# A Fourier attention layer and a mixture of experts on one core: two pairs of frequency bins are worked as one group, with the inverse length-64 stage for both at once

## The chip, the cores and the metric

The kernel runs on one core of a Trainium2 chip. The metric is the device time of one execution in microseconds (us). Each core has five engines that run their own instruction streams: PE (TensorE, matrix products; its weight loads are listed as PEld), DVE (VectorE), ACT (ScalarE), POOL (GpSimd) and SP (SyncE, which here issues the direct DMAs).

## The reference, cut to what matters

```python
def _attn_ref(x, w_r, w_i, b_r, b_i):            # x: 8 x 2496 x 256
    X = np.fft.rfft(x, axis=1)
    Yr = X.real @ w_r - X.imag @ w_i + b_r
    Yi = X.real @ w_i + X.imag @ w_r + b_i
    lam = 0.01
    Yr = np.sign(Yr) * np.maximum(np.abs(Yr) - lam, 0.0)   # Yi the same
    return np.fft.irfft(Yr + 1j * Yi, n=2496, axis=1)

def _moe_ref(x, modality_id, w_gate, modality_bias, w1, w2):   # x: 19968 x 256
    logits = x @ w_gate + modality_bias[modality_id]
    e_idx = np.argmax(logits, axis=1)            # one of 8 experts per token
    ...
    for e in range(E):
        h = np.maximum(x[mask] @ w1[e], 0.0)     # mask = e_idx == e
        out[mask] = gate_w[mask, None] * (h @ w2[e])
```

## The kernel before

The transform of length 2496 is split as 39 x 64. For each of the eight batches the attention stage first takes the length-39 DFT over x in 11 chunks (`s1_chunk`, L265 to L267; each chunk of x is split into a rounded high part on ACT or DVE and a remainder `x1l` on DVE, `s1_split`, L246 and L247) and sends it through DRAM (`scr`). Of the 39 bins 20 are kept, and they are worked two at a time: ten **pairs** per batch. A pair p goes through four steps on PE:

- `s2_pair` (L299): the length-64 DFT; ACT and DVE then cut the result into Us (a sum), Xh and Xl (L306 to L309).
- `mix_shared` (L329): two matmuls of the sums Us, on top of a bias that ACT has put into the PSUM tile `mx` (`mix_bias`, L317); then DVE adds the other bias and writes the second half of the tile (L330). The profile records each of these float32 matmuls twice.
- `mix_own` (L337): 12 matmuls of Xh and Xl into both halves of `mx`, so its first one has to wait for L330. Then `shrink`, the soft threshold (ACT L344, DVE L345).
- `is2_pair` (L360): the inverse length-64 stage, 16 matmuls that use half the rows of the array each (eight for either half), into two PSUM tiles, which DVE and ACT copy to `z` (L363), 256 wide.

In the loop over p of `build` the order is: sums of pair p+1, length-64 DFT of p+2, own half of p+1, inverse stage of p. After the ten pairs come the **pivots** of the batch: 22 rounds of `pivot` (L373, then ACT L378 and DVE L379) and `is1` (the inverse length-39 stage, L385 to L387, result copied by ACT or DVE, L388), with the s1 chunks of batch b+2 between them. A pair stage and its pivots make up the batch; the next batch's first sums stand behind the last pivot.

Beside that run: the **routing** of the batch before (`Route`: logits, softmax and ranks on DVE, its two sets of small matmuls on PE), which ends in 22 indirect DMAs that scatter a batch's tokens to `xs` in DRAM (`scatter`, L548, on POOL), one after each pair or two pivots; and the split of the experts' weights (`SplitWeights.step`: load `wr` on SP, rounded copy `wh` on ACT L994, remainder `wl` on POOL or DVE L995, two stores on SP, and the load for a later step). In the last two batches `rt.scatter(J)` issues whatever scatters are left, and behind those of batch 6's pivots `fence` (L592), a DMA on SP, waits for all of them before any expert may read `xs`.

Then come the experts (`Experts`): per tile of 256 tokens load `xt` from `xs`, `prep` (transposition on DVE L795, rounded copy on ACT L799, remainder `xl` on POOL L800) and `ffn` (L820, L850). PE's, ACT's, DVE's and POOL's streams follow the order in which the code is written (`manual_schedule`), with `prep` of the first tiles written into the end of the last batch; SP's order is left to a scheduler.

Of the kernel before, what the change touches and what calls it, by code (L numbers as in the profile page):

```python
# [27 lines left out]
J = 22  # L28
# [100 lines left out]
class Attn:  # L129
# [163 lines left out]
    def s2_pair(self, b, p, at):  # L293
# [10 lines left out]
        xh = self.w2.tile([128, 2, 2, 128], F32R, tag="Xh", name=f"Xh_{b}_{p}")  # L304
        xl = self.w2.tile([128, 2, 2, 128], F32R, tag="Xl", name=f"Xl_{b}_{p}")
# [6 lines left out]
    def mix_bias(self, b, p):  # L312

        ps = self.ps.tile([128, 2, 256], F32, tag="y", name=f"mx_{b}_{p}")
        if b == self.nb - 1 and p in (1, 2):
            self.fill(ps)
        self.nc.scalar.copy(ps[:, 0, :], self.bias[:, 0, :])  # L317
        return ps
# [29 lines left out]
    def is2_pair(self, b, p, s):  # L348

        nc = self.nc  # L350
        if p == 0:
            self.z = self.w1.tile([128, 2 * N2, K1, 2], F32, tag="z", name=f"z_{b}")
        ps = [self.ps.tile([128, 512], F32, tag="z", name=f"zs_{b}_{p}_{i}")[:, :256].rearrange("p (c m) -> p c m", c=2)
              for i in range(2)]
        for c in range(2):
            for r in range(2):
                o = (2 * p + r) * 128
                for i in range(2):
                    rows = slice(64 * i, 64 * i + 64)
                    nc.tensor.matmul(ps[i][:, c, :], s[rows, r, c * 128:(c + 1) * 128], self.q[rows, o:o + 128],  # L360
                                     start=r == 0, stop=r == 1)
        for i, copy in enumerate((nc.vector.tensor_copy, nc.scalar.copy)):
            copy(self.z[:, :, 2 * p + i, :], ps[i].rearrange("p c (n r) -> p (c n) r", r=2))  # L363

# [636 lines left out]
def build(tc, I, out, nb):  # L1001
    nc = tc.nc
    with ExitStack() as outer:
        dp = outer.enter_context(tc.tile_pool(name="wsp", bufs=1, space=DRAM))
        wsp = dp.tile([E * 128, 8192], F32, name="wsp")
        with ExitStack() as ctx:
# [9 lines left out]
            def load(i):  # L1016
                if i < last:
                    ld[i], ins = at.a_load(*divmod(i, 10))
                    return ins

# [16 lines left out]

            def ahead(i):
                load(i + 4)
                s2(i + 2)  # L1040

# [30 lines left out]
            for c in range(ahead1):  # L1072
# [8 lines left out]
                if c == 3:  # L1081
                    s2(1)
                if c == 4:
                    bias(1)
                    mix(0)
            ins = load(3)
            with tc.issue_after(ins.ins):
                at.s1_load(1, 5)

            state = None  # L1090
            routing = iter(())
            for b in range(nb):
                done = b == nb - 1
                for p in range(10):
                    i = 10 * b + p
                    due = state == "pe"

                    if p or not b:
                        shared(i + 1)
                    if b == 0:  # L1100
                        if p % 2 == 0 and p < 8:
                            with tc.issue_after(ins.ins):
                                if p < 6:
                                    at.table_load("m", p // 2 + 2)
                                at.table_load("q", p // 2 + 1)
                        ins = load(i + 4)
                        s2(i + 2)
                        if p == 9:
                            sw.load()
                            sw.load()  # L1110
                        if p == 3:
                            late = [rt.consts(), at.consts_last()]
                        if p in (3, 6):
                            with tc.issue_after(ins.ins):
                                for g in late:
                                    next(g, None)
                        for c in (2 * p + ahead1, 2 * p + ahead1 + 1):
                            if c < 11 and nb > 1:
                                at.s1_chunk(1, c, 2)
                    elif p > 0:  # L1120
                        ahead(i)
                    if p == 1 and b > 0:
                        rt.load_ids(b)
                    if p in (1, 2, 3, 5, 7, 9) and b + 2 < nb:
# [95 lines left out]
```

## Time and profile before

| | |
|---|---|
| median of 3 runs | 1563.2 us (1559.21 to 1564.9) |
| the profiled execution | 1560.42 us, its span 1558.7 us |
| mean granted clock of TensorE | 0.989 of full speed |
| attention stage, to the first L820 | 654.6 us |
| pair stage and pivots of a middle batch | 50 us and 26.5 us |
| experts | from 654.6 us to the end |

A row of the timeline names start, duration, engine, line, what is written and read, how many alike, and in brackets how long the engine had been idle and what released it. Waits are summed by the line that waited and the line that it waited for. PE's records overlap in time, as matmuls are pipelined: what one costs is read from the starts of rows, not from durations.

### The profile page before, as it was taken

Reading aid. Unit: us, or ns where it says so; the run is one execution under the profiler, and the core shown is the slowest. Engines: PE = TensorE matmul, PEld = TensorE weight load, DVE = VectorE, ACT = ScalarE, POOL = GpSimd, SP = SyncE. Lnnn points to the kernel's source line nnn. Section 1 sums busy time; section 2 is a strip of 40 time slices with the busy share of each in tenths; the row PEclk is TensorE's granted clock in tenths of the full one; section 3 lists DMA queues with packets and bytes.
Section 4 is the critical chain, followed back from the end, with each engine's and each line's share of the span. In section 5 each row is a group of like instructions: output and inputs, shape, how many; then the busy total and the mean of one; then the engine's idle time right before and its main releaser. Section 6 shows DMA issues by size and latency. Waiting matters only on the chain. (4 is left out here: it accounts for less than half of the span.)

```text
span 1558.7 us, 35171 instructions
## 1 busy us (share of the span) xinstructions
PE 1490.7 (96%) x12458; PEld 1423.3 (91%) x12458; DVE 723.9 (46%) x1586; ACT 662.6 (43%) x1415; POOL 513.5 (33%) x511
## 2 busy tenths in 40 slices
PE   4899999999999999899999999999999999999998
PEld 2788888888888888899999999999999999999998
DVE  3666666666666676444333333333333333333332
ACT  2466666666666555523232322232323222233232
POOL 0001444444443453524632233223232232223232
PEclk8999999999999999999999999999999999999999
DMA  7857686867685756633342523652225228625440
GB/s 198 242 171 265 193 268 198 266 201 256 207 261 175 233 178 220 187 97 71 90 121 48 159 46 95 217 154 47 51 51 158 42 53 278 233 50 171 142 152 29
DMA packets 289718, 244.57 MB, mean 157 GB/s; under 512 B 208448, under 2 KB 243980, under 8 KB 285289
## 3 DMA queue, kind: packets, MB, share of 16 engines
q1 hardware_dynamic: 270549, 200.73, 44.9%
q0 software_dynamic: 18992, 41.58, 8.1%
q8 instruction: 99, 1.62, 0.4%
q14 instruction: 78, 0.64, 0.1%
HBM read 432.83 MB, written 100.08 MB: 342 GB/s over the span
## 5 line engine op out<-in xcount | busy, mean ns | idle before, releaser
L850 PE MATMUL y<-w,hh 128*128 128x256 f32 x2496 | 432.5, 277 | 0.3 <-DMA w<-wsp 0.3
L820 PE MATMUL h<-xh,w 128*128 128x256 f32 x2496 | 402.3, 278 | 3.4 <-DMA w<-wsp 3.4
L850 PEld LDWEIGHTS y<-w,hh 128*128 128x128 f32 x2496 | 377.1, 188 | 0.9 <-ACT xh L799 0.4
L850 PE MATMUL y<-w,hl 128*128 128x256 f32 x1248 | 346.3, 277 | 0.1
L820 PEld LDWEIGHTS h<-xh,w 128*128 128x128 f32 x2496 | 338.8, 189 | 3.6 <-issue 3.6
L823 DVE SCALAR_TENSOR_TENSOR hl<-h,hh 128x512 fp32r<-128x512 f32 x312 | 209.3, 689 | 226.2 <-ACT hh L822 223.1
L863 POOL DMA_INDIRECT out<-o,ix x161 | 158.8, 986 | 426.7 <-ACT o L842 393.8
L820 PE MATMUL h<-xl,w 128*128 128x256 f32 x1248 | 244.7, 278 | 0.0
L822 ACT ACTIVATE hh<-h 128x512 fp32r<-128x512 f32 x312 | 178.3, 596 | 149.9 <-PE h L820 148.3
L850 PEld LDWEIGHTS y<-w,hl 128*128 128x128 f32 x1248 | 234.2, 188 | 0.8 <-DVE hl L823 0.3
L820 PEld LDWEIGHTS h<-xl,w 128*128 128x128 f32 x1248 | 189.3, 189 | 0.0
L840 DVE TENSOR_SCALAR o<-y,xt 128x256 f32<-128x256 f32 x78 | 37.7, 484 | 314.6 <-ACT o L842 310.5
L842 ACT ACTIVATE o<-y,xt 128x256 f32<-128x256 f32 x78 | 37.1, 476 | 343.2 <-PE y L850 343.2
L800 POOL TENSOR_TENSOR xl<-tr,xh 128x512 fp32r<-128x512 f32 x78 | 101.2, 1298 | 188.0 <-ACT xh L799 188.0
L337 PE MATMUL mx<-wmix,Xh 128*128 128x256 f32 x640 | 107.1, 289 | 15.4 <-DVE mx L330 11.8
L548 POOL DMA_INDIRECT xs<-x1b,si x88 | 87.9, 999 | 93.7 <-ACT u L344 38.5
L548 POOL DMA_INDIRECT xs<-x,si x88 | 88.0, 1000 | 73.6 <-ACT ph L378 30.2
L373 PE MATMUL pv<-pv,z 128*120 128x136 f32 x704 | 110.2, 281 | 1.4 <-DVE t_onea L686 0.8
L337 PEld LDWEIGHTS mx<-wmix,Xh 128*128 128x128 f32 x640 | 85.6, 188 | 27.1 <-DVE mx L330 26.4
L995 POOL TENSOR_TENSOR wl<-wr,wh 128x512 fp32r<-128x512 f32 x46 | 58.6, 1274 | 155.3 <-ACT wh L994 149.8
L373 PEld LDWEIGHTS pv<-pv,z 128*120 128x120 f32 x704 | 98.7, 185 | 7.8 <-ACT z L363 1.8
L379 DVE TENSOR_TENSOR pl<-pv,ph 120x264 fp32r<-120x264 f32 x176 | 75.8, 431 | 61.4 <-ACT ph L378 56.7
(191 smaller groups left out, 2111.9 us busy)
## 6 DMA issues: line engine op xcount, KB each, us to landing
w<-wsp SPq DMA_DIRECT2D x166, 2048.0 KB
a<-scr SPq DMA_DIRECT2D x80, 256.0 KB
xt<-xs SPq DMA_DIRECT2D x624, 32.0 KB
wr<-in_moe_w SPq DMA_DIRECT2D x64, 256.0 KB
wsp<-wh SPq DMA_DIRECT2D x64, 256.0 KB
wsp<-wl SPq DMA_DIRECT2D x64, 256.0 KB
scr<-ev SPq DMA_DIRECT2D x98, 160.0 KB
x<-in_x SPq DMA_DIRECT2D x96, 156.0 KB
```

What stands on the lines that cost most here:

```text
L337: self.nc.tensor.matmul(ps[:, i, :], t[:, c, 1 - i, :], self.w[:, i, c, lo, :], start=False, stop=n == len(ops) - 1, skip_group_check=True)
L373: nc.tensor.matmul(ps[:PK, c * 128:c * 128 + D // 2 + E], self.z[:, o:o + 3, :, :].rearrange("p n k r -> p (n k r)"), self.pv[:, c, :], st ...
L379: nc.vector.tensor_sub(pl, ps[:PK, :GC], ph)
L548: i = self.nc.gpsimd.indirect_dma_start(out=self.xs, out_offset=bass.IndirectOffsetOnAxis(ap=si[:, k:k + 1], axis=0), in_=rows, in_offset= ...
L800: nc.gpsimd.tensor_sub(xl, tr, xh)
L820: nc.tensor.matmul(ps[:, q, :], w1[:, lo, c, f * 128:(f + 1) * 128], x[:, c, :], start=n == 0, stop=n == 5)
L822: nc.scalar.activation(hh[:, 2 * p:2 * p + 2, :], ps, AF.Relu)
L823: nc.vector.scalar_tensor_tensor(hl[:, 2 * p:2 * p + 2, :], ps, 0.0, hh[:, 2 * p:2 * p + 2, :], ALU.max, ALU.subtract)
L840: nc.vector.tensor_scalar_mul(o[:, s, :], y[s], gate)
L850: nc.tensor.matmul(y[s], lhsT, w2[:, lo, f, :], start=n == 0, stop=n == 23)
L863: ins = self.nc.gpsimd.indirect_dma_start(out=self.out, out_offset=bass.IndirectOffsetOnAxis(ap=ix, axis=0), in_=o, in_offset=None, bounds ...
L995: eng.tensor_sub(lo, raw, hi)
```

## The change

Five groups g of two pairs take the place of ten pairs. With m = 10b + 2g + 2 a group issues: sums of m, sums of m+1, length-64 DFT of m+2, own half of m, own half of m+1, DFT of m+3, and the inverse stage of m-2 and m-1 in one go (32 half-height matmuls, one 512-wide copy to z by ACT and one by DVE). Xh and Xl get a third buffer, s a fourth. The bias tiles for the next batch's first group are written during the last pivots. Splits of x are written at other places, three times per batch two chunks per group: the first ahead of the DFT of m+2, the second behind the inverse stage. Scatters stand one behind each own half, two for some in the last two batches, and the weight steps come as up to two per group. The start of the program is written out anew, and so are the two sums ahead of the last `is1` of a batch.

```diff
-        xh = self.w2.tile([128, 2, 2, 128], F32R, tag="Xh", name=f"Xh_{b}_{p}")
-        xl = self.w2.tile([128, 2, 2, 128], F32R, tag="Xl", name=f"Xl_{b}_{p}")
+        xh = self.w3.tile([128, 2, 2, 128], F32R, tag="Xh", name=f"Xh_{b}_{p}")
+        xl = self.w3.tile([128, 2, 2, 128], F32R, tag="Xl", name=f"Xl_{b}_{p}")
...
-        s = self.w2.tile([128, 2, 256], F32, tag="s", name=f"s_{b}_{p}")
+        s = self.w4.tile([128, 2, 256], F32, tag="s", name=f"s_{b}_{p}")
...
-    def is2_pair(self, b, p, s):
...
+    def is2_group(self, b, g, ss):
...
+        ps = [self.ps.tile([128, 2, 2, 128], F32, tag="z", name=f"zs_{b}_{g}_{i}") for i in range(2)]
+        for h, s in enumerate(ss):
+            for c in range(2):
+                for r in range(2):
+                    o = (2 * (2 * g + h) + r) * 128
+                    for i in range(2):
+                        rows = slice(64 * i, 64 * i + 64)
+                        nc.tensor.matmul(ps[i][:, h, c, :], s[rows, r, c * 128:(c + 1) * 128], self.q[rows, o:o + 128],
+                                         start=r == 0, stop=r == 1)
+        z = self.z.rearrange("p n (k i) r -> p k i n r", i=2)
+        for i, copy in enumerate((nc.scalar.copy, nc.vector.tensor_copy)):
+            copy(z[:, 2 * g:2 * g + 2, i], ps[i].rearrange("p h c (n r) -> p h (c n) r", r=2))
...
+            s2(2)
+            mix(0)
+            bias(2)
+            mix(1)
+            bias(3)
+            s2(3)
...
-                for p in range(10):
-                    i = 10 * b + p
...
+                for g in range(5):
+                    m = 10 * b + 2 * g + 2
+                    if g or not b:
+                        shared(m)
+                        route()
+                        shared(m + 1)
+                    ins = load(m + 2) or ins
+                    ins = load(m + 3) or ins
...
+                    chunks = ((), (0, 1), (2, 3), (4, 5), ())[g] if b + 2 < nb else ()
...
+                    for c in chunks[:1]:
+                        at.s1_split(b + 2, c)
+                    route()
+                    s2(m + 2)
+                    steps = (b > 0) * min(2, max(0, (7 if b < 5 else 6) - 2 * g))
+                    if steps:
+                        sw.step(nc.gpsimd)
...
+                    mix(m)
+                    rt.scatter(1 if b < nb - 2 or g < 3 else 2, at.mark)
+                    if not due:
+                        route()
+                    mix(m + 1)
+                    rt.scatter(1 if b < nb - 2 or g < 2 else 2, at.mark)
...
+                    if g < 4:
+                        bias(m + 2)
...
+                    s2(m + 3)
+                    if g < 4:
+                        bias(m + 3)
+                    if steps > 1:
+                        sw.step(nc.gpsimd)
+                    route()
+                    at.is2_group(b, g, (ss.pop(m - 2), ss.pop(m - 1)))
+                    for c in chunks[1:]:
+                        at.s1_split(b + 2, c)
+                    route()
...
+                    if j == (20 if b + 2 < nb else J - 1):
+                        bias(10 * b + 12)
+                        bias(10 * b + 13)
...
-                bias(10 * b + 11)
-                shared(10 * b + 11)
-                ahead(10 * b + 10)
+                shared(10 * b + 12)
+                shared(10 * b + 13)
```

On PE, in batch 3 around pair 6 (mx_6 is the PSUM tile of pair 6, s_3_7 the length-64 DFT of pair 7, zs the inverse stage), before:

```order
L329 MATMUL mx_6_3866<-wmix_r,Us_6_3851 128x256 x2
L299 MATMUL s_3_7_3913<-c_m,a_7_3763 128x2x64 x4
L337 MATMUL mx_6_3866<-wmix,Xh_6_3852 128x256 x4
L337 MATMUL mx_6_3866<-wmix,Xl_6_3853 128x256 x2
L337 MATMUL mx_6_3866<-wmix,Xh_6_3852 128x256 x4
L337 MATMUL mx_6_3866<-wmix,Xl_6_3853 128x256 x2
L360 MATMUL zs_5_0_3958<-c_q,s_5_3881 128x128
```

and in the changed kernel (mx_7 belongs to pair 7):

```order
L329 MATMUL mx_6_3739<-wmix_r,Us_6_3682 128x256 x2
L329 MATMUL mx_7_3753<-wmix_r,Us_7_3746 128x256 x2
L299 MATMUL s_3_8_3810<-c_m,a_8_3798 128x2x64 x4
L337 MATMUL mx_6_3739<-wmix,Xh_6_3683 128x256 x4
L337 MATMUL mx_6_3739<-wmix,Xl_6_3684 128x256 x2
L337 MATMUL mx_6_3739<-wmix,Xh_6_3683 128x256 x4
L337 MATMUL mx_6_3739<-wmix,Xl_6_3684 128x256 x2
L337 MATMUL mx_7_3753<-wmix,Xh_7_3747 128x256 x4
```

Between the sums of pair 6 and its own half stood one DFT; now the sums of pair 7 stand there as well, and no inverse stage stands between the two own halves.

On DVE at the same place (L247 writes x1l, a split of x for batch 5; L330 is the bias that the own half needs; L308 and L309 cut the next DFT; L345 is the threshold; L363 the copy to z), before:

```order
L247 TENSOR_TENSOR x1l_1_3905<-x_0_3639,x1h_1_3904 117x512
L330 TENSOR_TENSOR mx_6_3866<-mx_6_3866,bias 128x256
L308 TENSOR_TENSOR Us_7_3918<-Us_7_3918,s_3_7_3913 128x256
L309 TENSOR_TENSOR Xl_7_3920<-s_3_7_3913,Xh_7_3919 128x512
L345 SCALAR_TENSOR_TENSOR s_6_3952<-mx_6_3866,u_6_3951 128x512
L363 COPY z_3600<-zs_5_0_3958 128x128x2
L247 TENSOR_TENSOR x1l_2_3971<-x_1_3710,x1h_2_3970 117x512
L330 TENSOR_TENSOR mx_7_3937<-mx_7_3937,bias 128x256
```

and in the changed kernel, where the copy to z is L364:

```order
L364 COPY z_3634<-zs_1_1_3766 128x2x128x2
L247 TENSOR_TENSOR x1l_1_3786<-x_0_3543,x1h_1_3785 117x512
L504 SCALAR_TENSOR_TENSOR oh_0_3789<-fr_0_3737,rm_0_3763 117x176
L330 TENSOR_TENSOR mx_6_3739<-mx_6_3739,bias 128x256
L330 TENSOR_TENSOR mx_7_3753<-mx_7_3753,bias 128x256
L247 TENSOR_TENSOR x1l_2_3807<-x_1_3665,x1h_2_3806 117x512
L308 TENSOR_TENSOR Us_8_3815<-Us_8_3815,s_3_8_3810 128x256
L309 TENSOR_TENSOR Xl_8_3817<-s_3_8_3810,Xh_8_3816 128x512
L345 SCALAR_TENSOR_TENSOR s_6_3843<-mx_6_3739,u_6_3842 128x512
L345 SCALAR_TENSOR_TENSOR s_7_3862<-mx_7_3753,u_7_3861 128x512
```

Here each L330 had one split ahead of it; now a group's two L330 share one split ahead of them (with the 512-wide copy to z), and the second split follows them.

On POOL at the end of batch 7's pivots (L548 is one scatter, a count stands behind it; L463 to L465 belong to batch 7's routing; L800 is the first expert tile's remainder xl), before:

```order
L548 DMA xs<-x1b,si_0_8021 162048x264 x6
L463 TENSOR_TENSOR b_7_8284<-omid_8282,mb 117x176
L464 TENSOR_TENSOR b_7_8285<-mid_8279,mb 117x176
L465 TENSOR_TENSOR b_7_8284<-b_7_8284,b_7_8285 117x176
L548 DMA xs<-x1b,si_0_8021 162048x264 x2
L800 TENSOR_TENSOR xl_8756<-tr_8753,xh_8755 128x512
L548 DMA xs<-x1b,si_0_8021 162048x264 x12
L800 TENSOR_TENSOR xl_8800<-tr_8797,xh_8799 128x512
```

and in the changed kernel:

```order
L548 DMA xs<-x1b,si_0_8080 162048x264 x2
L463 TENSOR_TENSOR b_7_8118<-omid_8116,mb 117x176
L464 TENSOR_TENSOR b_7_8119<-mid_8113,mb 117x176
L465 TENSOR_TENSOR b_7_8118<-b_7_8118,b_7_8119 117x176
L548 DMA xs<-x1b,si_0_8080 162048x264 x20
L800 TENSOR_TENSOR xl_8596<-tr_8593,xh_8595 128x512
L800 TENSOR_TENSOR xl_8640<-tr_8637,xh_8639 128x512
```

The first L800 stood ahead of 12 of the 22 scatters; now it stands behind all of them, eight of which are issued in a row after the last pivot. In DVE's order the first expert tile's transposition (L795) has moved from ahead of the first pivot's L379 to behind the last one's. At the border of batches 6 and 7 the same holds: 20 scatters in a row stand ahead of batch 7's first weight step, where 14 stood.

## Rows read from the trace of the kernel before

**Rows 1.** The page's part 1: busy us, share of the span, instructions

```profile
PE 1490.7 (96%) x12458; PEld 1423.3 (91%) x12458; DVE 723.9 (46%) x1586; ACT 662.6 (43%) x1415; POOL 513.5 (33%) x511
```

**Rows 2.** Windows, batch 2's pairs: length, busy (x) by engine, clock, DMA share, GB/s

```profile
207.55:257.50 49.95, 47.42 (x411) 42.46 (x411) 31.20 (x73) 29.19 (x65) 20.27 (x21) 1.00 0.74 235
```

**Rows 3.** Waits of the whole program: us in total, times, longest us

```profile
PEld mx L337 <- DVE mx L330: 26.4, 57, 1.3
...
PE mx L337 <- DVE mx L330: 11.8, 25, 1.1
...
PE mx L329 <- ACT mx L317: 7.0, 8, 0.9
```

**Rows 4.** Timeline of PE in batch 3: start, duration, what

```profile
299.71 0.38 PE L329 MATMUL mx<-wmix_r,Us 128*128 128x256 f32 x1
299.93 1.05 PE L299 MATMUL s<-c_m,a 128*128 128x128 f32 x8
300.74 0.71 PE L337 MATMUL mx<-wmix,Xh 128*128 128x256 f32 x4
...
316.79 0.74 PE L337 MATMUL mx<-wmix,Xh 128*128 128x256 f32 x4
...
317.59 0.62 PE L337 MATMUL mx<-wmix,Xh 128*128 128x256 f32 x4
318.04 0.39 PE L337 MATMUL mx<-wmix,Xl 128*128 128x256 f32 x2
318.36 1.16 PE L360 MATMUL zs<-c_q,s 64*128 64x128 f32 x16
319.45 1.13 PE L329 MATMUL mx<-wmix_r,Us 128*128 128x256 f32 x4
320.42 1.05 PE L299 MATMUL s<-c_m,a 128*128 128x128 f32 x8
```

**Rows 5.** Timeline of all engines around the next pair's own half

```profile
317.43 0.63 ACT L994 CAST wh<-wr 128x512 fp32r<-128x512 f32 x1
...
319.85 0.43 SPq L982 DMA_DIRECT2D wr<-in_moe_w  x1
...
320.53 0.69 DVE L247 TENSOR_TENSOR x1l<-x,x1h 117x512 fp32r<-117x512 f32 x1 [0.26 <-ACT x1h L246]
321.14 0.42 DVE L330 TENSOR_TENSOR mx<-mx,bias 128x256 f32<-128x256 f32 x1
...
321.62 0.54 PEld L337 LDWEIGHTS mx<-wmix,Xh 128*128 128x128 f32 x4 [0.34 <-DVE mx L330]
```

**Rows 6.** Timeline of PE from batch 1's pivots to batch 2

```profile
206.36 0.28 PE L387 MATMUL i<-pl,c_g 120*117 120x264 f32 x1
207.55 1.13 PE L329 MATMUL mx<-wmix_r,Us 128*128 128x256 f32 x4 [0.91 <-ACT mx L317]
```

**Rows 7.** Timeline of PE, batch 7 to the experts

```profile
583.43 1.13 PE L329 MATMUL mx<-wmix_r,Us 128*128 128x256 f32 x4 [0.68 <-ACT mx L317]
...
628.66 1.62 PE L373 MATMUL pv<-pv,z 128*120 128x136 f32 x12 [0.60 <-ACT z L363]
634.93 0.57 PE L385 MATMUL i<-ph,c_g 120*117 120x264 f32 x1 [4.65 <-ACT ph L378]
...
652.51 0.63 PE L373 MATMUL pv<-pv,z 128*120 128x136 f32 x4
...
654.59 0.41 PE L820 MATMUL h<-xh,w 128*128 128x256 f32 x2
```

**Rows 8.** Windows, batch 7's first pivots; columns as in rows 2

```profile
630.00:640.00 10.00, 5.35 (x27) 5.14 (x26) 2.83 (x7) 3.16 (x9) 6.27 (x6) 0.66 0.57 112
```

**Rows 9.** Timeline of all engines in the same stretch

```profile
633.19 0.71 DVE L795 STREAM_TRANSPOSE tr<-xt 128x512 f32<-128x512 f32 x1 [4.68 <-DMA xt<-xs]
...
634.68 1.28 POOL L800 TENSOR_TENSOR xl<-tr,xh 128x512 fp32r<-128x512 f32 x1 [2.16 <-ACT xh L799]
...
637.45 0.99 POOL L548 DMA_INDIRECT xs<-x1b,si  x1 [0.30 <-issue]
```

More of the change, by code (lines that the diff above doesn't have):

```diff
@@ L346, in shrink @@
         return s
-    def is2_pair(self, b, p, s):
+    def is2_group(self, b, g, ss):
         nc = self.nc
-        if p == 0:
+        if g == 0:
             self.z = self.w1.tile([128, 2 * N2, K1, 2], F32, tag="z", name=f"z_{b}")
[L353 to L363, printed above, removed]
+        ps = [self.ps.tile([128, 2, 2, 128], F32, tag="z", name=f"zs_{b}_{g}_{i}") for i in range(2)]
[10 more added lines that the diff above has]
+            copy(z[:, 2 * g:2 * g + 2, i], ps[i].rearrange("p h c (n r) -> p h (c n) r", r=2))
     def pivot(self, b, j):
@@ L1019, in load @@
                     return ins
+                return None
             def s2(i):
@@ L1088, in build, with route @@
                 at.s1_load(1, 5)
+                at.table_load("m", 2)
+            s2(2)
[4 more added lines that the diff above has]
+            s2(3)
             state = None
             routing = iter(())
+            def route(n=1):
+                nonlocal state
+                for _ in range(n):
+                    if state != "pe":
+                        state = next(routing, None)
             for b in range(nb):
                 done = b == nb - 1
[L1094 to L1108 removed]
+                for g in range(5):
[6 more added lines that the diff above has]
+                    ins = load(m + 3) or ins
+                    if b == 0:
+                        with tc.issue_after(ins.ins):
+                            if g < 2:
+                                at.table_load("m", g + 3)
+                            if g < 4:
+                                at.table_load("q", g + 1)
+                            if g == 1:
+                                late = [rt.consts(), at.consts_last()]
+                            if g in (1, 3):
+                                for t in late:
+                                    next(t, None)
+                        if g == 4:
@@ L1109, in build @@
                             sw.load()
                             sw.load()
[L1111 to L1117, printed above, removed]
+                    elif g == 0:
+                        rt.load_ids(b)
@@ L1118, in build @@
+                    if steps:
+                        sw.step(nc.gpsimd)
+                    route()
+                    due = state == "pe"
+                    if b == 0:
+                        for c in range(4 * g + ahead1, 4 * g + ahead1 + 2):
                             if c < 11 and nb > 1:
                                 at.s1_chunk(1, c, 2)
[L1120 to L1123, printed above, removed]
@@ L1124, in build @@
-                    if p in (1, 2, 3, 5, 7, 9) and b + 2 < nb:
-                        with tc.issue_after(ins.ins):
-                            at.s1_load(b + 2, (1, 2, 3, 5, 7, 9).index(p))
-                    if b > 0 and p < (7 if b < 5 else 6):
-                        sw.step(nc.gpsimd)
-                    if p < 9:
-                        bias(i + 2)
-                    mix(i + 1)
-                    rt.scatter(1 if b < nb - 2 or p < 5 else 2, at.mark)
+                    mix(m)
```

27 lines of the change are left out of this document (14 added, 13 removed).

## The prediction

> **What bounds the kernel now.** I first read the busy times of the page: PE is busy for 96% of the span [rows 1], so only what makes PE's starts denser can count; DVE, ACT and POOL are all under half. The experts, two thirds of the span, are issued by the same code, so I looked at the attention stage. In its windows DVE and ACT are busy for some 60% and the DMA engines for 74% of a pair stage of 49.95 us [rows 2]; none is full, so PE is held by single waits. The list of waits names them: the first matmul of an own half waits for DVE's bias L330, 26.4 us in 57 waits by the weight loads, and a batch's first sums wait for ACT's bias tile, 8 times [rows 3].
>
> PE's timeline then says what a wait costs. A pair's period is 316.79 to 321.62, 4.83 us. The DFT takes 0.81 where its successor is ready (299.93 to 300.74) but 1.20 here (320.42 to 321.62) [rows 4, 5]: 0.39 lost, where the row shows 0.34 of idle. Behind the wait PE fills up slowly: four matmuls of the own half are 0.45 apart from the next (317.59 to 318.04), 0.1125 each, so six should take 0.68, and the first six take 0.80 (316.79 to 317.59) [rows 4]. That is 0.12 more, 0.51 in all, and 4.32 without the wait. DVE's rows show the cause: L330 starts at 321.14, right behind a split of x of 0.69, and its own 0.42 lie before the load at 321.62 [rows 5].
>
> **The change, part by part.**
>
> *The wait for L330.* Between the sums of pair m and its own half now stand the sums of m+1 (0.97, 319.45 to 320.42) and a DFT (0.81) [rows 4]; L330 needs 0.42 [rows 5]. Alone it is covered. For the second own half the cover is larger by the first. So I take out all of it: 26.4 us shown plus 57 times the 0.17 that a row leaves out (0.51 less 0.34), **36.1 us**.
>
> What remains is the split that the order still has ahead of a group's L330, in groups 2 to 4. From the end of the inverse stage to the own half PE has 0.97 + 0.97 + 0.81 = 2.75 us of work. ACT's copy to z (512 wide; the nearest row is ACT's 512-wide cast, 0.63), ACT's cast of x (0.63 as well), DVE's split 0.69 and L330 0.42 come one behind the other: 2.37, and with some 0.1 to 0.2 for each of four hand-overs 2.8 to 3.2 [rows 4, 5]. So it ends about when PE arrives, 0 to 0.5 late. With routing operations of DVE between them in group 2 I take 0.7 us per batch in the six batches that split ahead (the upper bound, 0.5 in all 35 groups of the first seven batches, is a rival below): **-4.2 us**.
>
> *Fewer inverse stages.* 80 blocks become 40. Each block costs something at its edges. The last two matmuls before it take 0.32 (318.04 to 318.36) where 0.225 is due by the spacing above; the block itself 1.09 (318.36 to 319.45) where eight full slots are 0.90; and the sums behind it 0.97, where the fourth of them takes 0.22 (299.71 to 299.93), so the first has 0.09 extra [rows 4]. Together 0.10 + 0.19 + 0.09 = 0.38 us; 40 blocks fewer give **15.2 us** (11, if 0.10 of it belongs to each slot and not to the edge).
>
> A rule speaks against this. In the own half four weight loads take PEld 0.54 us, 0.135 each [rows 5], yet its matmuls follow each other at 0.1125 [rows 4]: loads run under full-height matmuls in flight. The Trainium skill ("TensorE: Matmul & The Clock Gate", section Part 3: Packing small matmuls) states that weight loads overlap matmuls in flight only where their row groups differ. By that rule the own half would be the place with open loads and the half-height inverse stage the one without, and the sum below would be 1534 instead of 1519; the trace disagrees in the own half. I keep 15.2, and hold the case that merging saves nothing as a rival.
>
> *The border between batches.* The bias tiles are now written during the last pivots, so the first sums need not wait. They began 1.19 after the last L387 (206.36 to 207.55), where a next matmul takes 0.12 [rows 6]: 1.07 in each of seven borders, **7.5 us**.
>
> *New waits outside the steady state.* At the start, DFTs, sums and own halves now follow each other directly, so one chain of cuts (ACT copy, ACT cast 0.63, DVE add 0.42; about 1.4 [rows 5]) lies open, and the tables loaded behind other transfers may cost 1 more: **-2.4 us** (0 to -4). In the last two batches no s1 chunks cover the copy to z, which is 512 wide now: **-0.8 us**.
>
> *The end of batch 7.* Before, batch 7 runs from 583.43 to the experts at 654.59; its pivots, from 628.66, contain a wait of 4.65 [rows 7]. DVE stands there at the first tile's transposition, which waits for xt [rows 9], and the clock was granted at 0.66 over these 10 us, that is 6.8 us at the lower of its levels 1.2 and 2.4 GHz [rows 8]; at most 5.1 us of work behind the wait ran so, which cost some 2.2. The transposition has moved behind the last pivot, so **+6.9 us**.
>
> But eight scatters that stood in the pair stage now stand behind the last pivot, and the first tile's remainder (L800) behind them. A scatter takes 0.99 and 0.30 more to issue [rows 9]. Counted from the last pivot (652.51 before): 0.8 to its own scatter, nine times 1.29, and 1.28 for L800 [rows 7, 9] make 13.7. Before, the experts began 2.1 behind that pivot (654.59) [rows 7]; the first two products need only the high part. So PE waits about 11.4 us, and as in the rows above the clock falls and costs 2.2 behind it: **-13.6 us**. At the border of batches 6 and 7 eight more scatters end 10.3 later; SP's fence waits for them, and the weight loads that SP issues behind it come late. A step's load is issued 2.4 behind its cast (317.43 to 319.85) [rows 5] and used two steps later, so it had a lead of 2 x 4.83 - 2.4 = 7.2 us; ACT will hold at a cast, and PE behind it, for 10.3 less a lead of 5.9 to 7.2, **-3.4 us** (0 to -10.3). The three together are -10.1 us.
>
> The sum: 36.1 + 15.2 + 7.5 - 4.2 - 2.4 - 0.8 - 10.1 = 41.3 us. Against the profiled execution's 1560.4 us that is 1519.1. The median shown lies 2.8 above that execution, inside the spread of the three; I say **1520**.
>
> **The rivals.**
>
> *The tail hides.* If the scatters run faster when nothing else asks for POOL, or SP puts other work ahead of the fence, the 13.6 and the 3.4 stay away: 1502. For it: POOL is idle for most of the attention stage [rows 1]. Against: 0.30 between two scatters was no wait but issue [rows 9].
>
> *The wait for L330 stays by half.* If each group of the first seven batches keeps 0.5 us, 35 x 0.5 = 17.5 in place of 4.2: 1533. For it: the chain above ends within a few tenths of PE's arrival, and PE arrives earlier in a faster batch.
>
> *The edges are not edges.* If what I read as edges of the inverse stage belongs to its half-height slots, because loads there hide no better in one long block than in two short ones, the 15.2 is no gain: 1535. For it: eight full slots of that stage take 1.09 where the DFT's eight take 0.81. Against: the last two matmuls ahead of it and the first behind it are slow too [rows 4]. (The rule of the Trainium skill's "TensorE: Matmul & The Clock Gate" named above points to this case.)
>
> *The DMA engines become the bound.* The same bytes in 43.4 instead of 49.95 us raise their share from 0.74 to 0.85 [rows 2]. If they cannot pass 0.80 in the mean, a pair stage stays 2.8 us longer in six batches: 1536. If they stay at 0.74, it keeps its length: 1559, no change. Against: no PE wait on a transfer is among the large ones.
>
> *Weight loads come late, and it gets slower.* With two steps per group of about 8.3 us the lead falls from 7.2 to 8.3 - 2.4 = 5.9 [rows 5]. ACT's stream is in order: a cast that waits holds the bias tiles and thresholds behind it, and PE waits for those. The gain is eaten where a load takes 5.9 + 41/32 = 7.2 us (32 groups carry steps), and it is slower beyond 7.45. At 8 us: 32 x 2.1 = 67 us, 1587. Against: by the waits of before, a load lands within 7.2.
>
> **How the numbers follow.** My forecast has a chance of 0.50 (its own range 1513 to 1526), the hidden tail 0.14, the half wait 0.15, the edges 0.06, the DMA bound 0.10 (of which no change 0.05), late weight loads 0.03; 0.02 is left for mixtures. A measurement of this kernel tells about 0.5%, 8 us, from no change. Faster is all but the no change and the late loads: 0.92; same 0.05; slower 0.03. The range reaches from a little below the hidden tail, 1499, over the half wait, the edges and the milder DMA case to 1543, which leaves out the no change, the late loads and some tenth of the rest.
>
> **What would show it.** Right, if in the trace after: L330 is gone as a releaser of own halves or down to a few us; inverse stages stand in blocks of 32 that take about 2.0 us; the first sums of a batch start 0.12 behind the last L387; a middle batch has come down from 76.5 to about 69; and the experts' third product waits some 11 us for L800 behind eight scatters 1.3 apart, at a lower granted clock afterwards. Wrong, if own halves still wait behind splits, if ACT's casts L994 wait for transfers in the steady state, or if the scatters at the end overlap or come earlier than PE.

## The result and the profile after

The changed kernel takes 1536.5 us (median of 4 runs, 1535.4 to 1537.0) against 1564.1 us; the ratio is 0.983, with an interval of 0.980 to 0.985. That lies inside the range that was given, and 16.5 us above the 1520 forecast: of 43 us forecast, 27.5 came.

The list of waits of the changed kernel (us in total, times, longest) shows which waits went and which came, beside [rows 3]:

```profile
PE h L820 <- POOL xl L800: 10.3, 1, 10.3
...
ACT ev L270 <- DMA scr<-ev: 7.3, 1, 7.3
...
PE mx L329 <- ACT mx L317: 5.7, 2, 4.8
...
PE mx L329 <- DVE Us L308: 3.3, 3, 1.7
...
PEld mx L337 <- DVE mx L330: 2.2, 3, 1.3
```

L330 held the own halves for 26.4 us in 57 waits and now holds them for 2.2 in 3. New are the wait of the experts for L800, as forecast, and two that were not: ACT waits 7.3 us for a store of ev, and PE 4.8 us for a bias tile of ACT, once.

PE's timeline of the changed kernel at the border to batch 3 and in two of its groups:

```profile
280.49 0.28 PE L387 MATMUL i<-pl,c_g 120*117 120x264 f32 x1
280.61 1.95 PE L329 MATMUL mx<-wmix_r,Us 128*128 128x256 f32 x8
...
291.55 1.05 PE L299 MATMUL s<-c_m,a 128*128 128x128 f32 x8
292.36 0.72 PE L337 MATMUL mx<-wmix,Xh 128*128 128x256 f32 x4
...
295.27 1.05 PE L299 MATMUL s<-c_m,a 128*128 128x128 f32 x8
296.25 2.06 PE L360 MATMUL zs<-c_q,s 64*128 64x128 f32 x32
298.24 1.99 PE L329 MATMUL mx<-wmix_r,Us 128*128 128x256 f32 x8
300.07 1.05 PE L299 MATMUL s<-c_m,a 128*128 128x128 f32 x8
301.42 0.73 PE L337 MATMUL mx<-wmix,Xh 128*128 128x256 f32 x4 [0.29 <-DVE mx L330]
```

The first sums of a batch start 0.12 us behind the last L387, where it was 1.19 [rows 6]. A group without a wait is, from start to start, sums 1.83 (298.24 to 300.07), DFT 0.81, two own halves 2.91 (292.36 to 295.27), DFT 0.98 and inverse stage 1.99: 8.52 us. Two pairs without a wait were 8.82 (4.41 each, and not the 4.32 of the prediction: see the account of the wait for L330 below), so a group saves 0.30 us. The last row has the one wait for L330 that this batch still shows, in group 2, where DVE has routing work besides the split.

Where the time went, stage by stage, by the starts of rows in both timelines:

| | before | after | difference in the stretch | the prediction's terms for it |
|---|---|---|---|---|
| first pivot of batch 0 | 105.95 | 117.75 | +11.8 | -2.9 |
| first pivot of batch 7 | 628.66 | 595.25 | -45.2 | -45.1 |
| first L820 | 654.59 | 615.32 | -5.9 | -6.9 |
| end of the span | 1558.7 | 1534.8 | +15.4 | +13.6 |

(The terms: at the start 3.4 for batch 0's seven waits, 1.9 for its inverse blocks, less 2.4; in the last two rows 4.65 + 2.2 and 11.4 + 2.2; all others in the second.) The differences add up to the 23.9 us between the two profiled executions, the terms to 41.3. A middle batch has come down from 76.5 to 69.4 us. The stretch from batch 0's pivots to batch 7's changed by what was forecast for it; the start lost 14.7 us more than its terms say, the end 2.8.

What happened at the start is seen in a timeline of all engines of the changed kernel:

```profile
72.42 1.37 SPq L281 DMA_DIRECT2D scr<-ev  x3
...
73.83 0.42 SPq L415 DMA_DIRECT2D tri_st<-in_c_tri  x1
...
78.46 0.33 SPq L197 DMA_DIRECT2D st_g<-in_c_g  x1
...
79.85 1.50 SPq L281 DMA_DIRECT2D scr<-ev  x3
...
84.83 0.59 ACT L270 COPY ev<-s 120x512 f32<-120x512 f32 x1 [7.33 <-DMA scr<-ev]
85.31 0.69 ACT L344 ACTIVATE u<-mx,nlam 128x512 f32<-128x512 f32 x1
...
87.41 0.38 ACT L317 COPY mx<-bias 128x256 f32<-128x256 f32 x1
...
87.84 3.78 PE L329 MATMUL mx<-wmix_r,Us 128*128 128x256 f32 x8 [4.84 <-ACT mx L317]
```

The copies of s1 chunks (L270) go through three buffers of the tag ev, and two staging tiles for late constants, tri_st and st_g, come from the same three. In the new order these are taken ahead of batch 1's last chunk. SP's load of st_g then stands until the store that was issued at 72.42 has landed, the next store of ev waits behind it on SP until 79.85, and ACT's last copy of batch 1 needs that store's buffer. Behind this copy ACT has the threshold and the bias tile that PE waits for. The windows around it (length, busy by engine, granted clock, DMA share, GB/s) show the clock as well:

```profile
80.00:90.00 10.00, 5.16 (x47) 4.49 (x46) 2.78 (x5) 4.36 (x10) 0.00 (x0) 0.85 0.57 178
90.00:100.00 10.00, 10.00 (x80) 9.32 (x80) 6.21 (x12) 4.72 (x11) 0.00 (x0) 0.81 0.57 178
```

PE is idle for half of the first window, and the granted clock is 0.85 and 0.81, by these shares 3.0 and 3.8 us at the lower of its two levels (1.2 and 2.4 GHz): about 2.9 us more by the stages behind the wait (the eight sums take 3.57 us instead of 1.83, and so on).

The end went as forecast, in the timeline of all engines and a window of the changed kernel:

```profile
612.08 0.63 PE L373 MATMUL pv<-pv,z 128*120 128x136 f32 x4
612.14 0.99 POOL L548 DMA_INDIRECT xs<-x1b,si  x1 [0.30 <-ACT x L388]
...
615.32 0.50 PE L820 MATMUL h<-xh,w 128*128 128x256 f32 x2 [0.99 <-ACT xh L799]
...
623.78 0.99 POOL L548 DMA_INDIRECT xs<-x1b,si  x1 [0.30 <-issue]
624.80 1.26 POOL L800 TENSOR_TENSOR xl<-tr,xh 128x512 fp32r<-128x512 f32 x1
...
626.12 0.80 PE L820 MATMUL h<-xl,w 128*128 128x256 f32 x2 [10.30 <-POOL xl L800]
```

```profile
620.00:630.00 10.00, 3.88 (x19) 3.88 (x20) 0.65 (x2) 0.60 (x1) 5.12 (x5) 0.52 0.42 132
```

From the last pivot to L800's end are 14.0 us (13.7 were worked out), PE waits 10.3 (11.4), and the clock of the window is 0.52.

### The profile page after: what moved, and what is told of

It reads as the page before. It is cut to its first block, busy times and chain, and to the rows that moved or that the text cites. A ratio compares the mean times of both kernels' runs of the same rounds, so it can differ in the third digit from the quotient of the medians.

```text
span 1534.8 us, 35125 instructions
## 1 busy us (share of the span) xinstructions
PE 1469.2 (96%) x12458; PEld 1420.7 (93%) x12458; DVE 722.9 (47%) x1546; ACT 657.8 (43%) x1375; POOL 510.7 (33%) x511
## 3 DMA queue, kind: packets, MB, share of 16 engines
q1 hardware_dynamic: 270549, 200.73, 45.2%
## 5 line engine op out<-in xcount | busy, mean ns | idle before, releaser
L820 PE MATMUL h<-xh,w 128*128 128x256 f32 x2496 | 403.7, 278 | 4.5 <-DMA w<-wsp 3.4
L820 PEld LDWEIGHTS h<-xh,w 128*128 128x128 f32 x2496 | 340.2, 189 | 5.0 <-issue 3.6
L820 PE MATMUL h<-xl,w 128*128 128x256 f32 x1248 | 245.7, 278 | 10.3 <-POOL xl L800 10.3
L820 PEld LDWEIGHTS h<-xl,w 128*128 128x128 f32 x1248 | 189.8, 189 | 10.5 <-POOL xl L800 10.5
L800 POOL TENSOR_TENSOR xl<-tr,xh 128x512 fp32r<-128x512 f32 x78 | 101.0, 1294 | 187.5 <-ACT xh L799 187.4
L548 POOL DMA_INDIRECT xs<-x1b,si x88 | 87.8, 998 | 83.8 <-ACT ph L378 30.5
L548 POOL DMA_INDIRECT xs<-x,si x88 | 87.8, 998 | 69.1 <-ACT u L344 25.4
L379 DVE TENSOR_TENSOR pl<-pv,ph 120x264 fp32r<-120x264 f32 x176 | 76.0, 432 | 55.6 <-ACT ph L378 51.3
L799 ACT CAST xh<-tr 128x512 fp32r<-128x512 f32 x78 | 48.5, 622 | 107.6 <-DVE ix L802 93.6
```

The lines of the kernel that those rows point to most:

```text
L379: nc.vector.tensor_sub(pl, ps[:PK, :GC], ph)
L548: i = self.nc.gpsimd.indirect_dma_start(out=self.xs, out_offset=bass.IndirectOffsetOnAxis(ap=si[:, k:k + 1], axis=0), in_=rows, in_offset= ...
L799: nc.scalar.copy(xh, tr)
L800: nc.gpsimd.tensor_sub(xl, tr, xh)
L820: nc.tensor.matmul(ps[:, q, :], w1[:, lo, c, f * 128:(f + 1) * 128], x[:, c, :], start=n == 0, stop=n == 5)
```

## The experiments

The runs below stand on another chip than the first result, the last on a third; each ratio is against the kernel before on the same chip. On the second chip batch 7 (counted from batch 6's first pivot to its own) and its pivots were slower for every kernel with the group order (about 66 and 25 us instead of 61.5 and 20; the variants of the kernel before took 68.6 to 70.0 for this batch 7 where that kernel took 66.0), so they are compared with the changed kernel there: 0.9848 (0.983 to 0.987), 1548.5 us.

**The changed kernel again (e0).** No edit.

> The changed kernel itself, to stand beside the following runs on one chip. Both theories: 0.983 of the kernel before. Its batch 7 and the pivots behind it took 61.5 and 20.1 us in its first profile, and 66.5 and 24.4 to 25.2 us in the two variants run on the other chip; if they take 61.5 and 20.1 here as well, the variants lost there by themselves, if about 66 and 24, the chip or the execution is the reason.

Measured 0.9848; batch 7 takes 65.7 us and its pivots 25.8. So this comes with the chip or the execution, and the variants did not lose there by themselves.

**Two inverse blocks (e1).**

```diff
+            if h:
+                between()      # the DFT of m+3, its bias, a weight step, routing
...
-                    s2(m + 3)
...
+                    at.is2_group(b, g, (ss.pop(m - 2), ss.pop(m - 1)), between)
```

> The changed kernel with the inverse stage of a group again in two blocks of 16 matmuls, the first ahead of the DFT of pair m+3, the second behind it; the copies to z stay 512 wide and everything else stays. If an inverse block costs 0.38 us at its edges, as the prediction has it, 40 more blocks cost 15 us (about 1552 us). If the edges hardly exist, as the stage sums of the changed kernel suggest (inverse stage, sums, DFT and own half together are down by only 0.65 us per batch against unwaited stages of before), it costs 5 us or less (about 1541). If the merged block saves nothing at all, the time stays at 1536.5.

Measured 1.0012 (0.9996 to 1.003): 25.8 us above the changed kernel. Its timeline of PE and its waits for L330:

```profile
302.96 1.16 PE L362 MATMUL zs<-c_q,s 64*128 64x128 f32 x16
304.05 1.16 PE L299 MATMUL s<-c_m,a 128*128 128x128 f32 x8
305.14 1.16 PE L362 MATMUL zs<-c_q,s 64*128 64x128 f32 x16
306.23 2.29 PE L329 MATMUL mx<-wmix_r,Us 128*128 128x256 f32 x8
```

```profile
PEld mx L337 <- DVE mx L330: 9.2, 18, 1.0
```

Two blocks take 2.18 us instead of 1.99, and the DFT between them 1.09 instead of 0.98; in batch 1's sum of starts the own halves grow by 0.30, 0.06 in a group. Together 0.36 to 0.37 us for each block more, about 15 us: the edge is as large as predicted. The other 11 us are for the most part waits, with one block less behind the DFT: by the starts of rows the DFTs ahead of own halves are longer by 6.9 us in all than in e0, and the sums by 2.6. So an inverse block does cost 0.37 us. The change as made saved 0.30 of it per group (8.82 less 8.52), 12 us of 15.2 forecast, since a group now pays 0.17 where the DFT stands ahead of the inverse stage (0.98 against 0.81), and most of its own matmuls are spaced at 0.118 us where they were at 0.113. (The "0.65 us per batch" of the expectation counts from the 4.32 that the prediction gives a pair.)

**Staging tiles a group later (e2).**

```diff
-                            if g == 1:
+                            if g == 2:
                                 late = [rt.consts(), at.consts_last()]
-                            if g in (1, 3):
+                            if g in (2, 4):
```

> The changed kernel with one thing moved: the two staging tiles for late constants (tri_st, st_g), which share the three ev buffers of the s1 copies, are taken in batch 0's group 2 instead of group 1, behind the last chunk of batch 1; their use moves from group 3 to group 4. Theory: the second staging load waits on SP for a store of ev, the next store of ev stands behind it, ACT waits 7.3 us for the buffer, PE 4.8, and the clock is granted low for some 6 us behind that. Then 7 to 8 us go (about 1529 us), and ACT shows no wait for scr<-ev above 1 us. Rival: the start is late because its chain of DFT, sums and own halves is open (waits for DVE's L308), and the stall only uses up time that PE would have lost anyway: 0 to 3 us go (1533 to 1537).

Measured 0.9829 (0.980 to 0.986), 1541.8 us: 3 us less than the changed kernel by the ratios, 6.7 by the medians. In the trace the start is 9.0 us shorter (first pivot at 102.8 us behind the first matmul instead of 111.8), the wait of ACT for the store is gone, and of PE's waits at the start this one is left:

```profile
PE mx L329 <- DVE Us L308: 3.1, 2, 1.7
```

The granted clock is 1.00 from 80 to 100 us, where it was low. So the cause of the stall is shown, and what it cost at its place; in the total the gain is not clear of noise by itself (the two intervals overlap); together with two more repairs it is (e7).

**The start reordered (e6).** The sums of pair 1 one chunk later, and two chunks of batch 1 ahead of the first group's sums.

```diff
-                if c == 4:
+                if c == 5:
                     shared(1)
...
             s2(3)
+            at.s1_chunk(1, 6, 2)
+            at.s1_chunk(1, 7, 2)
...
-                            if c < 11 and nb > 1:
+                            if g and c < 11 and nb > 1:
                                 at.s1_chunk(1, c, 2)
```

> The changed kernel with the open chain at the start covered: the sums of pair 1 one s1 chunk later, and two s1 chunks of batch 1 between the DFT of pair 3 and the sums of pairs 2 and 3. If these sums' waits for DVE's L308 (1.3 and 1.7 us) and the low clock behind the first are a loss of their own, 4 us go beside the changed kernel of the same call; if they only precede the stall of ACT on the ev buffer, which ends at the same moment, 0 to 1 us.

Measured 0.9855 (0.984 to 0.988): nothing. The start is 1.3 us shorter, as the second theory has it: the sums behind the stall start at 88.3 us where they started at 88.5.

**First xl on DVE (e3).**

```diff
-        nc.gpsimd.tensor_sub(xl, tr, xh)
+        (nc.gpsimd if i else nc.vector).tensor_sub(xl, tr, xh)
```

> The changed kernel with the first expert tile's remainder xl (L800) computed by DVE instead of POOL, so that it doesn't stand behind the eight scatters; nothing else changes. Theory: the scatters only cost because that one subtraction stands behind them: the wait of 10.3 us before the third product falls to about 1, the low clock behind it goes, and the time falls by 11 to 12 us (about 1525). Rival: the experts' first tiles are held by something else that is late as well (the second tile's xl on POOL, the loads of xt and of weights behind the fence on SP), and 0 to 6 us are gained.

Measured 0.9864 (0.984 to 0.989): no gain. The wait for L800 is gone, and the first two expert tiles still take 31.6 us where the changed kernel takes 35.7 and the kernel before 23.7. Its timeline of all engines shows what stands behind:

```profile
635.43 0.99 POOL L548 DMA_INDIRECT xs<-x1b,si  x1 [0.30 <-issue]
...
638.32 5.29 SPq L763 DMA_DIRECT2D w<-wsp  x4
...
645.76 0.47 PE L820 MATMUL h<-xh,w 128*128 128x256 f32 x2 [2.01 <-DMA w<-wsp]
```

and SP's own waits from 600 to 660 us say what held the load of weights (L763):

```profile
SPq L763 <- DMA xs<-x1b,si: 8.7, 1, 8.7
```

So SP issues the load of the second tile's weights only when the scatters have read x1b; it fits this that the weights are placed where x1b lay. The scatters cost by two ways, and the prediction had one. e9 and e12 test it.

**Three repairs (e7).** The edits of e2, e6 and e3 together.

> The changed kernel with three repairs at once: the staging tiles a group later, the start as in the run before this one, and the first tile's xl on DVE. If the losses stand in separate places they add up: 8 + 2 to 4 + 5 to 12 us less than the changed kernel of the same call (about 0.968 of before). If what is gained at the start is given back at the end, because the experts' first tiles and the fence wait for transfers, 8 us or less (about 0.978).

Measured 0.9794 (0.978 to 0.981), 1539.5 us: 8.5 us less than the changed kernel. The start takes 100.0 us instead of 111.8; the first two tiles 32.0, as in e3. At the end little is gained. (The start spreads by some us from profile to profile: it takes 100.0 to 103.1 in the four variants that have e2's edit, e2, e7, e9 and e12, and 109.5 to 111.8 in the six group-order profiles without it. So e2's edit is worth 7 to 9 us, and e6's, in either set, nothing that stands out.)

**Scatters sooner (e10), and with the three repairs (e9).**

```diff
-                        rt.scatter(1, at.mark)
+                        rt.scatter(1 if b < nb - 2 else 2, at.mark)
```

> The changed kernel with this last edit alone: two scatters behind every second pivot in the last two batches. xl of the first tile still stands on POOL behind all of them. POOL then works the 20 scatters back to back at 1.29 us, which ends about 4 to 5 us sooner at the experts and at the fence: the wait for xl falls from 10 to 5 or 6 us, and the time by 4 to 8 us (0.980 to 0.982). If the scatters can't go back to back (each ordered behind a pivot's ACT copy, or held by DMA), 0 to 2 us.

> The changed kernel with the three repairs of the earlier run (staging tiles later, start, first xl on DVE) and, in the last two batches, two scatters instead of one behind every second pivot, so that eight fewer stand behind the last one. Theory: behind the wait for xl stood a second one of the same cause; the loads of the second tile's weights are placed where the scatters' source lay and start only when the last scatter has read it. The scatters then end 4 to 6 us sooner and so do the weights, in batch 7 the fence as well: 4 to 7 us less than with the three repairs (0.975 to 0.977 of before). Rival: PE's second wait is for loads that are slow by themselves, and the time stays at 0.979.

Measured 0.9936 (0.991 to 0.996) and 0.9875 (0.985 to 0.990): 14 us slower than the changed kernel, 13 slower than the three repairs. In e9 the first two expert tiles take 24.4 us, like the kernel before, and SP's wait for scatters before the second tile's weights is down to 0.8, so the wait for weights is indeed the scatters'. But the pivots of the last batch take 37.6 us in e10 and 38.9 in e9 where the changed kernel has 25.8, and those of batch 6 are longer too. A timeline of all engines of e10 in batch 7's pivots:

```profile
623.52 0.99 POOL L548 DMA_INDIRECT xs<-x1b,si  x1 [0.30 <-issue]
...
624.40 0.63 PE L373 MATMUL pv<-pv,z 128*120 128x136 f32 x4
...
630.00 0.99 POOL L548 DMA_INDIRECT xs<-x1b,si  x1 [0.30 <-issue]
630.64 0.38 ACT L378 CAST ph<-pv 120x264 fp32r<-120x264 f32 x1 [6.76 <-remote]
...
631.36 0.57 PE L385 MATMUL i<-ph,c_g 120*117 120x264 f32 x1 [6.33 <-issue]
```

PE has finished a pivot by 625.0, and ACT takes it up at 630.6, while POOL issues a scatter every 1.3 us; "remote" says that the profile names no releaser on this core. Both theories of e10 failed: the wait for xl fell from 9.7 to 0.8 us, and more was lost in a place neither named.

**Routing sooner (e12).** The three repairs, and in the last two batches two routing steps at a time.

```diff
-                for _ in range(n):
+                for _ in range(n * (2 if b >= nb - 2 else 1)):
```

> The changed kernel with the three repairs (0.9794 of before) and, in the last two batches, two steps of the routing at each place that had one, so that a batch's scatters are ready by group 3 again: 8 instead of 2 then stand in batch 7's pair stage, 12 in the pivots at the old spacing, and 2 instead of 8 behind the last pivot (4 at the border of batches 6 and 7). Theory: the end of the attention stage costs what stands behind the last pivot, first by xl, then by the second tile's weights, and packing scatters into the pivots only costs because they follow each other without a pause there. Then the first two expert tiles take 24 us instead of 32, the pivots keep their 26, and the time is 6 to 9 us below the three repairs (0.974 to 0.976). If the added DVE work of the routing holds the own halves, or scatters in the pair stage hold ACT as those in the pivots did, nothing is gained (0.979 or more).

Measured 0.9726 (0.971 to 0.974), 1520.2 us against 1562.9 us: the best kernel of this study. The first two tiles take 26.5 us, the pivots 20.1, at the price of 2.8 us in batch 6 (the DFT's stage grows from 9.1 to 11.7 us by waits for L330). It ran on the third chip, where batch 7 is as short as in the first result, so its distance to the three repairs is not all the edit's; the 5.5 us at the first tiles are.

**Parts alone, on the kernel before: splits behind the own half (e4), the bias early (e5), both (e8).**

```diff
                     mix(i + 1)
+                    if p > 3 and b + 2 < nb:
+                        at.s1_split(b + 2, p - 4)
...
-                    if 2 < p < 9 and b + 2 < nb:
-                        at.s1_split(b + 2, p - 3)
```

```diff
+                    if j == (20 if b + 2 < nb else J - 1):
+                        bias(10 * b + 11)
...
-                bias(10 * b + 11)
                 shared(10 * b + 11)
```

> The kernel before with one part of the change alone: each split of x for batch b+2 is issued behind the own half and the threshold of an iteration instead of at its end, so that DVE reaches the bias L330 before it. If the splits ahead of L330 are what the own halves wait for, the 26 us of waits fall to about 8 (the pairs without a split keep 0.3 or less each) and the time by 15 to 25 us (about 1540 to 1548). If L330 is late by itself, because 0.81 us of DFT do not cover its 0.42 us and the hand-overs, or because other work of DVE takes the split's place, the waits stay and the time falls by less than 6 us (above 1557).

> The kernel before with one other part of the change alone: the bias tile of the next batch's second pair is written during the last pivots instead of behind them. If ACT's bias behind the last pivot is all that a batch's first sums wait for, 1.0 us goes at each of seven borders and the time falls by 7 us (0.9955 of before); if the sums then wait for something else (Us, or the PSUM tile that the bias now holds earlier), less than 2 us (0.999).

> The kernel before with both small moves, no groups: splits of x behind the own half and the threshold, and the bias tile of the next batch's second pair during the last pivots. If the two gains stand in separate places they multiply: 0.9936 x 0.9938 = 0.987 of before, within 0.3% of the whole change (0.9848). If both fill the same idle time, 0.992 or more.

Measured 0.9936 (0.992 to 0.996), 0.9938 (0.992 to 0.996) and 0.9906 (0.988 to 0.993), so 10, 10 and 14.8 us. What waits for L330 in e4, and for the bias in e5:

```profile
PEld mx L337 <- DVE mx L330: 17.1, 39, 0.9
```

```profile
PEld mx L329 <- ACT mx L317: 1.1, 2, 0.9
```

In e5 the first sums start 0.12 us behind the last L387 at five of seven borders, where it was 1.19, as its first theory has it. In e4 L330 still holds 39 own halves for 17.1 us of the 26.4, more than the first theory allows (about 8) and less than the second (all of it). Its timeline of all engines shows what took the split's place:

```profile
303.30 0.18 DVE L534 TENSOR_TENSOR si<-sl,inv 117x22 int32<-117x22 f32 x1
303.40 0.42 DVE L330 TENSOR_TENSOR mx<-mx,bias 128x256 f32<-128x256 f32 x1
...
303.88 0.54 PEld L337 LDWEIGHTS mx<-wmix,Xh 128*128 128x128 f32 x4 [0.63 <-DVE mx L330]
```

L534 is an operation of the routing. Counted over all 80 L330, in the kernel before 37 of the 57 waits, 19.4 us, were behind an L330 that came directly behind a split, and in e4 33 of the 39, 14.8 us, behind one that came directly behind the routing. Where DVE had been idle before L330 (21 times in e4), an own half waited once. So one DFT does cover an L330 that DVE can start at once; what it does not cover is other work of DVE ahead of it, split or routing. In the changed kernel, with the sums of a second pair as cover besides, 20 of the 80 L330 still stand directly behind routing, and three loads wait. A batch is shorter than in the kernel before on the first chip by about 1.3 us in e4, by 0.1 to 0.8 in e5 and by 2.2 to 2.6 in e8: the moves do add up there. In the total they do not: to the last matmul of their tiles, e8's experts take 905 us from the first L820 where e4's take 897 (see the last section).

## Why the prediction was right, and where it was wrong

*The wait for L330* was the main term (36.1 us), and right in place: 2.2 us are left of 26.4. Its size was read too high. The prediction adds 0.17 to each row's wait, 0.12 of it because PE fills up slowly behind a wait, and so puts a wait at 0.51. But an own half without a wait starts as slowly, in PE's timeline of the kernel before:

```profile
300.74 0.71 PE L337 MATMUL mx<-wmix,Xh 128*128 128x256 f32 x4
301.28 0.39 PE L337 MATMUL mx<-wmix,Xl 128*128 128x256 f32 x2
301.51 0.62 PE L337 MATMUL mx<-wmix,Xh 128*128 128x256 f32 x4
```

Its first six matmuls take 0.77 us (300.74 to 301.51), those behind the wait 0.80. So the wait of the prediction's rows cost 0.39 + 0.03 = 0.42, and a pair without it takes 4.41. By the starts of all rows the DFTs ahead of the 57 waits run 28.7 us over their 0.81; with 0.03 more for each, 30 us were there to win. Its cause was not the splits alone: in 17 cases the routing stood directly ahead of L330, and e4, which only moves the splits, took a third of the wait away.

*New waits for L330 behind splits* were put at 4.2 us, in the six batches that split ahead; batches 1 to 5 show less, 0.2 to 0.6 us each by the starts of rows, mostly in group 2 (another 1.8 us are in batch 7).

*Fewer inverse stages* was near its size: 15.2 us, of which about 12 came by the rows without a wait (0.30 for each of 40 groups). The edge of a block was right (0.37 us in e1 against 0.38). What "40 blocks fewer" left out is the new edge: the order now has the DFT, and not the own half, ahead of the block and pays 0.17 there. The slower spacing of own matmuls took about 0.1 us more per group. The rival that merging saves nothing fell with e1: more blocks do cost. The rule of the Trainium skill ("TensorE: Matmul & The Clock Gate", section Part 3: Packing small matmuls) pointed to that rival; it also disagrees with the own half's rows here, where full-height loads of 0.188 us each run under matmuls spaced at 0.113 to 0.118 us.

*The border* was right: 1.07 us went in six of seven (e5 shows it alone). At the seventh PE now waits 0.6 us for DVE a step earlier.

*The start* is the step that failed, and most of the distance to the forecast. The prediction put it as "one chain of cuts lies open, and the tables loaded behind other transfers may cost 1 more: -2.4 us (0 to -4)". The open chain was there (waits of 1.3 and 1.7 us for L308), but the price came from a resource that it did not look at: the staging tiles take two of three ev buffers, and moving their load ahead of a chunk made SP, then ACT, then PE wait, and the clock fall. Taken by itself this cost 9.0 us at its place (e2; 7 to 9 over all profiles). The waits of the open chain can be taken away (e6) without a gain that stands out. Of the 14.7 us some 6 stay open: without the stall the start takes 100.0 to 103.1 us from the first matmul, where the kernel before takes 99.4 and 2.9 less were forecast.

*The end of batch 7* was right in mechanism and near in size: 14.0 us from the last pivot to L800 where 13.7 were worked out, and the pivots are shorter by 5.9 (6.9 forecast). The experts lost 15.4 us where the term was 13.6; 12.2 of it are in the first two tiles (35.9 against 23.7). What it missed is that this wait hid a second one: e3 took the first away and gained nothing, since the second tile's weights wait for the same scatters.

*The fence* was put at 3.4 us. In batch 7 of the changed kernel ACT stands 3.8 us before a weight step's cast (L994, the profile names no releaser), whose load SP issued behind the fence, and PE's inverse stage, sums and DFT behind it take 6.46 us instead of 4.63: 1.8 us.

Of the rivals, the DMA bound and late weight loads did not occur: no PE wait on a transfer is among the new ones in the middle batches, and batch 2's pair stage takes 45.5 us with the DMA engines at a share of 0.84, above the 0.80 of the milder case. The hidden tail did not either.

So the time came out within the range because the middle batches gave what was forecast, and above the forecast mostly because of the start. That the middle agrees to 0.1 us (45.2 of 45.1) is partly luck. Between the first pivots of batches 0 and 7, by the starts of rows, the wait for L330 gave 24.3 us (28.5 were forecast for this stretch, new waits taken off) and the borders 6.4 (7.5); the remaining 14.5, inverse stages, routing matmuls and what the fence took, stand against 9.1. The terms that were too high and those that were too low cancel.

## What to carry to other kernels

Where an edit moves a step of a start-up sequence, list every buffer ring that the step takes a tile from, staging tiles included, and follow who gets the same buffer next: here a load of constants moved past one chunk cost 7 to 9 us at its place. Merging stages saves the edges that vanish and not those that turn into others: write the order of stages down before and after, and count transitions. What a wait costs is read against the same stage without a wait in the same trace, slow start included. When a wait at a handover is taken away, look first for what else is released by the same late work; here the first tile's operand and the second tile's weights waited for the same scatters.

## What the runs showed of the hardware that was not expected

Matmuls of 256 columns go at two spacings in spells, with the same granted clock in the windows: about 0.113 and 0.118 us. The own halves of before are mostly at 0.113, those of the changed kernel at 0.118, and the DFT and the pivots keep theirs. In the experts the spells change from tile to tile (10.9 or 11.3 us per tile); 16% of the expert matmuls are at the slow spacing (0.116 us or more) in the kernel before, 19% in the changed one, 14% in e12 and 31% in e8, which makes about half of the 8 us by which e8's experts are longer than e4's. What starts a spell stays open.

On the second chip ACT took up PE's results 1.5 to 2.3 us late several times in batch 7's pivots of the changed kernel, and up to 6.8 us late when scatters followed each other without a pause (e10). In e10 the profile names no releaser for this wait; in the changed kernel it names the pivot's matmuls, which had ended by then; whether it is the transfers, the chip or something else was not settled. In the changed kernel's first profile, on the first chip, it does not occur.
